# A recurrent-memory attention block with its gradients: another issue order for the backward chain, and a fixed order for the last stage's first transfers

## The chip, the cores and the metric

The kernel runs on one core of a Trainium2 chip, in one launch. The metric is the time of that launch on the device in microseconds (us), and smaller is better. TensorE is called PE here, VectorE DVE, ScalarE ACT, GpSimd POOL and SyncE SP; PE, DVE, ACT and POOL compute, and SP, ACT and POOL issue DMA transfers from queues of their own.

## The reference

The forward pass adds three things: the input, an attention with a memory that is carried from segment to segment, and a squared-ReLU MLP. The attention and the MLP both read the layer-normalised input. The sequence has S = 2048 rows of D = 512 in bf16; there are 32 heads of 128, 64 segments of 32 rows, a memory of 8 rows and an MLP width of 1792.

```
mem = mem0
for s in range(64):
    h = concat([mem, xn[32*s : 32*s + 32]])          # 40 rows
    q, k, v = h @ Wq, h @ Wk, h @ Wv                 # 32 heads of 128
    p = softmax(mask(q @ k.T * 128 ** -0.5))
    o = (p @ v) @ Wo
    mem, out[s] = o[:8], o[8:]                       # the next segment starts from mem
y = x + out + (relu(xn @ w1 + b1) ** 2 @ w2 + b2)
```

The kernel returns y and, for a given gradient of y, the gradients of x, mem0, Wq, Wk, Wv, Wo, w1, b1, w2 and b2. The memory makes both directions chains: no segment's forward can end before the one ahead of it, and the gradient of a segment needs the gradient of the memory that the segment behind it received.

## The kernel before

**Stages.** The kernel first does the MLP and the layer norm (to about 267 us of the profiled span), then the rows of the memory (the "left" rows) of all blocks together, then the forward chain of 64 segments (to about 1200 us). It then does the backward of the memory rows' own part and the MLP weight gradients (to about 1435 us), then the backward chain, again 64 segments (about 1435 to 2431 us), and at the end the last stage, which forms the four attention weight gradients and the input gradient (from 2508 us).

**The backward chain.** A segment is a step; four steps make a block, sixteen blocks in all, and both are taken from the last to the first. `bwd(s)` makes the operations of a step and `left(b)` those of a block; each has a short name. In a step: `o0mm` and `o1mm` project the incoming gradient GT through Wo; `o0ev`, `o0fl` and `o0te` copy that out, transpose it and copy again (p = 0 and 1 are halves of the heads); `s0` and `s1` are the score gradients; `d10` to `d41` are the DVE operations of the softmax gradient, which end in gS; `tu0` and `tu1` turn gS into gST; `vp`, `kp` and `qp` are the outer products for the gradients of v, k and q in PSUM tile b_pp (two of them, `pp0` and `pp1`, which the three share in turn); `vea`, `kea0`, `qea1` and so on copy these out to gv, gk, gq (names with `l`, such as `kla0`, copy the memory rows' part, b_gkL); `vg`, `kg` and `qg` gather them through the transposed weights into ps_gR; `ra` and `rb` copy that to R; `ta` and `tb` transpose R into ps_sum; and `HT` adds the four groups into GT, which is what the next step starts from. `ldp`, `ldq`, `ldn`, `ldk` and `vtr` load the next step's data, `pb` and `vc` are POOL copies. A block's operations: `L.G0` to `L.I3` are the gathers (ps_RL) for the memory rows, `L.ra0` to `L.ra3` sum them, `L.ta`, `L.tb` and `L.xt` turn them into b_XL, `L.sl` and `L.sx` store, and `L.ktr`, `L.vtr` and `L.qtr` transpose the gradients gkL, gvL and gqL of the memory rows by DMA into gNat, which `L.kst`, `L.vst` and `L.qst` store to S_GL.

All of this is issued in the order written out by hand in `B_ORDER` (L1088 to L1103), inside a manual schedule in which no tool reorders anything: four strings, for the steps 0, 1, 2 and 3 of a block (called rows 0 to 3 here). Most of row 0 stands at the end of the fourth string, one block ahead, and the first string holds only how it ends. A `+` or `-` behind a name moves it to the block or step before or after. `ENGS` (L1104) says which copies ACT does; its second string names those of DVE. Each engine runs its own instructions in order, so an instruction that waits holds all behind it on its engine.

**The last stage** (L1393 to L1506) works through 16 groups of columns, `COLS`: each is 160 products of 128 x 128 by 128 x 512 (L1503), eight results in PSUM in the case of Wo (the first group, where all eight are run side by side) or one after another. A group of Wo's gradient needs a tile `gn` of the projected output rows (S_ON, S_OL; loaded by POOL, L1419 and L1425) and GOc, the gradient rows; the others need a `gn` transposed by DMA from S_GB on SP's queue (L1422) and HNc, the rows of the normalised input. `slot_side` makes GOc and HNc: four DMA transposes on ACT's queue (L1407) and four plain copies (L1410). `loads(i)` fetches the tile for group i, two groups ahead; there are three such tiles. `leave` copies a result out of PSUM through a tile wt (six buffers) and stores it from POOL's queue. Behind each group `input_rows` (L1441 to L1471) takes a block of the input's gradient: POOL loads XT (L1444) and XL, PE transposes XT into ps_rows (L1456) and DVE and POOL finish it.

**What sets the order here.** The tile framework lets a scheduler choose the order of this stage outside a manual schedule. A transpose by DMA on one queue waits until those issued from the other queue have all landed; a framework rule adds that wait. Two transposes that write the same tile name (gNat) wait for each other's reader.

Of the kernel before, what the change touches and what calls it, by code (L numbers as in the profile page):

```python
# [10 lines left out]
BF16 = mybir.dt.bfloat16  # L11
F32 = mybir.dt.float32
P = 128
# [13 lines left out]
def kernel(  # L27
# [27 lines left out]
    nc = tc.nc  # L55

    _, S, D = A_x.shape
    M = A_mem0.shape[1]
# [4 lines left out]
    L = M + SEG  # L63
# [26 lines left out]
    gflat = grad_out.flatten_outer_dims()  # L90
# [5 lines left out]
    dma = nc.sync.dma_start  # L96
# [5 lines left out]
    NB = NSEG // SPB  # L102
    HG = 4
    KH = H // HG
# [10 lines left out]
    S_XN = dram.tile([S, D], BF16, name="S_XN")  # L115
    S_GT = dram.tile([P, DC, S], BF16, name="S_GT")

    S_HT = dram.tile([P, DC, S], BF16, name="S_HT")
    S_HX = dram.tile([S // P, P, DC, P], BF16, name="S_HX")
    S_XL = dram.tile([P, DC, S // SEG * M], BF16, name="S_XL")  # L120
    S_GM = dram.tile([P, DC, S], BF16, name="S_GM")
# [19 lines left out]
    S_GL = dram.tile([NB, HG, SEG, 3, GW], BF16, name="S_GL")  # L141
# [15 lines left out]
    def sb(name, bufs, side=None):  # L157
        return tc.tile_pool(name=name, bufs=bufs, side=side, reuse_waits="tile")

    def psum(name, bufs):  # L160
        return tc.tile_pool(name=name, bufs=bufs, space=bass.MemoryType.PSUM, reuse_waits="tile")
# [8 lines left out]
    HT = htp.tile([P, DC, S], BF16, name="HT")  # L170
# [237 lines left out]
    def turned_heads(W):  # L408

        return lambda h: W[:, :, h * P:(h + 1) * P]  # L410
# [166 lines left out]
    def on_engines(act, vec):  # L577

        return dict([(n, acp) for n in act.split()] + [(n, vcp) for n in vec.split()])
# [43 lines left out]
    with sb("fw", 1) as fw, psum("fr", 4) as fr, psum("fpp", 1) as fpp, \  # L623
# [26 lines left out]
        def big(name):  # L650
            return fr.tile([P, 512], F32, name=name, tag="r")
# [285 lines left out]
    with sb("la", 2) as la, sb("ls", 2) as ls, sb("lo", 1) as lo_, sb("wg", 2) as wg, psum("lpp", 1) as lpp, psum("lr", 4) as lr:  # L937
# [84 lines left out]
        side, part = {}, {}  # L1022
# [53 lines left out]
        with tc.manual_schedule():  # L1076
# [3 lines left out]
            for b in range(NB + 1):  # L1080
                for nm in LB_ORDER:
                    k = nm.rstrip("-")
                    c = b - (nm != k)
# [2 lines left out]


    B_ORDER = (  # L1088
        "rb tb ta ldk HT",
        "L.H2 L.ktr L.gl+ klb1- o0mm o1mm kla1- L.ra1 vc- o0ev o0fl xt- o0te vp0 s0 d10 o1ev vla vea d20 vp1 o1fl vg0 "  # L1090
        "d30 o1te s1 vtr vlb d40 kp0 tu0 d11 d21 d31 veb d41 qp0 vg1 tu1 keb0 L.sl- kea0 qeb0 kg0 kla0 qea0 vc qp1 "
        "kp1 klb0 kla1 qea1 keb1 qeb1 kea1 ldq qg0 qg1 klb1 kg1 L.I2 ra rb tb ta pb L.kst HT",
        "xt- L.I3 o0mm ldn- o0ev o1mm o0fl o1ev L.vtr o0te vp0 L.ra2 L.G3 ldk- s0 vea vp1 d10 o1fl d20 vla L.vst vtr "
        "vg0 d30 d40 veb vtr+ tu0 kp0 o1te qp0 vc klb0 s1 L.qtr vg1 vlb keb0 qeb0 qea0 ldp d11 d21 d31 d41 kea0 qg0 "
        "tu1 kp1 ldq ldp+ kla0 ldk pb L.ldt+ kea1 qp1 ldn kg0 keb1 klb1 qea1 kg1 L.qst qeb1 qg1 rb L.H3 tb ra L.ra3 "
        "ta HT",
        "o0mm o0ev o1mm L.gs+ vc o0fl kla1- o1ev vp0 o1fl xt- vp1 L.ldv+ o0te o1te s0 vea d10 d20 veb d30 s1 d40 vlb "
        "vg0 tu0 L.I0+ kp0 L.vo1+ d11 d21 vla d31 ldq kea0 L.lq+ d41 klb0 kla0 qp0 keb0 qeb0 vg1 pb qea0 kg0 qg0 tu1 "
        "kp1 qp1 L.G0+ keb1 L.vo0+ kea1 qeb1 kg1 qea1 L.qo0+ qg1 ra rb L.H0+ L.ko0+ tb klb1 ta HT L.ta L.ra0+ L.tb "
        "o0mm+ kla1 o0ev+ o1mm+ o1ev+ ldn vp0+ o0fl+ vea+ vp1+ L.xt o1fl+ o0te+ vla+ veb+ o1te+ s0+ d10+ vg0+ d20+ "  # L1100
        "d30+ d40+ ldk xt L.qo1+ s1+ L.ldk+ vlb+ L.sx+ L.ko1+ tu0+ vg1+ kp0+ d11+ kea0+ d21+ keb0+ d31+ L.I1+ klb0+ "
        "qp0+ ldn+ L.G1+ L.G2+ d41+ qea0+ tu1+ kg0+ qeb0+ kla0+ qp1+ ldp+ qg0+ ldq+ vtr+ qea1+ kp1+ qeb1+ kea1+ ldp++ "
        "qg1+ pb+ keb1+ kg1+ ra+ L.H1+")  # L1103
    ENGS = on_engines(  # L1104
        "L.ra0 kea0 keb0 keb1 kla0 kla1 o0ev o1ev qea0 qeb0 rb vea veb vla vlb",
        "kea1 klb0 klb1 o0te o1te qea1 qeb1 ra")
    with sb("bq", 1) as bq, sb("bt", 1) as bt, sb("bs", 2) as bs, sb("be", 1) as be, psum("bpp", 1) as bpp, psum("br", 4) as br:
        G4 = {n: bq.tile([P, HG, KH, SPB, SEG], BF16, name="g" + n) for n in "vkq"}
        gS = bq.tile([P, KH, KW], BF16, name="gS")
# [28 lines left out]
        def left(b):  # L1138
            B_ = block(b)
            ps, st, o = {}, {}, {}  # L1140
            src = {"v": "gvL", "k": "gkL", "q": "gqL"}
            o["lq"] = lambda: dma(B_["gqL"][:], S_GQL[b])

            def following(f):

                return lambda: f(b - 1) if b > 0 else None
            for n, f in loads.items():
                o[n] = following(f)
            o["gs"] = lambda: dma(S_GM[:, :, b * P:(b + 1) * P], gts[b][:])
            for t, n in enumerate("qkv"):  # L1150
                for x in range(2):
                    def so(n=n, t=t, gs=slice(2 * x, 2 * x + 2) if n == "v" else slice(0, HG),
                           ks=slice(0, KH) if n == "v" else HALF[x]):
                        dma(S_GB[b, t][:, gs, ks], G4[n][:, gs, ks].rearrange("p g k j r -> p g k (j r)"))
                    o["%so%d" % (n, x)] = so

            jobs = [(turned_heads(Wqkv[t]), src[n], k) for t, n in ((2, "v"), (1, "k"), (0, "q")) for k in range(KH)]
            for i in range(4):
                for x, nm in enumerate("GHI"):
                    def G_(i=i, x=x):  # L1160
                        if ("R", i) not in ps:
                            ps["R", i] = big("ps_RL")
                            ps["n", i] = 0
                        ps["n", i] += 1
                        for m, (W, n, k) in enumerate(jobs[6 * i + 2 * x:6 * i + 2 * x + 2]):
                            for g in range(HG):
                                nc.tensor.matmul(ps["R", i][32 * g:32 * g + 32, :].rearrange("p (a b) -> p a b", b=P),  # L1167
                                                 lhsT=B_[n][:, k, g, :], rhs=W(g * KH + k), start=(ps["n", i] == 1 and m == 0),
                                                 stop=(ps["n", i] == 3 and m == 1), tile_position=(0, 32 * g))
                    o["%s%d" % (nm, i)] = G_  # L1170
                if i == 0:
                    o["ra0"] = lambda: ENGS["L.ra0"](B_["R4"][:], ps["R", 0][:])
                else:
                    o["ra%d" % i] = lambda i=i: nc.vector.tensor_tensor(out=B_["R4"][:], in0=ps["R", i][:],
                                                                        in1=B_["R4"][:], op=ALU.add)
            turn_ops(o, big, lambda: B_["R4"], st)

            def xt():
                st["XL"] = bt.tile([P, DC, SPB, M], F32, name="b_XL", tag="XL")
                left_sums(st["XL"], st["T"])  # L1180
            o["xt"] = xt
            o["sl"] = lambda: dma(S_XGL[b], st["XL"][:])

            for t, n in enumerate("qkv"):
                def nt(n=n):
                    st[n] = bt.tile([P, KH, P], BF16, name="gNat", tag="gNat")
                    nc.sync.dma_start_transpose(st[n][:], B_[src[n]][:].rearrange("p k g r -> p k (g r)"))
                o[n + "tr"] = nt
                o[n + "st"] = lambda n=n, t=t: dma(S_GL[b].rearrange("g r t c -> (g r) t c")[:, t, :],
                                                   st[n][:].rearrange("p k e -> p (k e)"))  # L1190

            o["sx"] = lambda: dma(S_XG[b], B_["XT"][:].rearrange("p c j r -> p c (j r)"))
            return o

        pre, gts, loads = {}, {}, {}
# [161 lines left out]
        with tc.manual_schedule():  # L1357
# [3 lines left out]
            for b in range(NB):  # L1361
                lefts.append(left(b))
# [34 lines left out]
    with sb("p5a", 1) as p5a, sb("p5h", 1) as p5h, sb("p5", 2) as p5, sb("p5g", 1) as p5g, \  # L1397
# [6 lines left out]

        def slot_side(t_, srcT, src):
            for dc in range(DC):
                nc.scalar.dma_start_transpose(t_[:, 0:NB, dc * P:(dc + 1) * P], srcT[:, dc, :])  # L1407
            lv = src.rearrange("(c q r) d -> c q r d", q=16, r=SEG)
            for c in range(NLC):
                nc.scalar.dma_start(t_[:, NB + c, :], lv[c][:, 0:M, :])  # L1410
            return t_

        def rows_of(i, g, blocks, left_):
# [19 lines left out]
        def loads(i):  # L1433
            if i < len(COLS):
                t, g = COLS[i]
                if t == 3:
                    got[i] = rows_of(i, g, None, lambda g: S_OL[:, g])
                else:
                    got[i] = rows_of(i, g, lambda b: S_GB[b, t], lambda g: S_GL[:, g, :, t, :])
# [40 lines left out]
        p5g.tile([P, 896], BF16, name="gap5")  # L1480
        GOc = p5g.tile([P, RC_ALL, D], BF16, name="GOc")
        side = p5h.tile([P, RC_ALL, D], BF16, name="HNc")
        loads(0)
        slot_side(GOc, S_GM, gflat)
        loads(1)
        slot_side(side, S_HT, S_XN[:])
        for i, (t, g) in enumerate(COLS):
            loads(i + 2)
            gn = got[i]
# [52 lines left out]
```

## Time and profile before

The median of three runs is 3085.69 us (3084.45 to 3087.76). One profiled execution spans 3081.8 us.

| what | us |
|---|---|
| PE busy | 2698.1 (88% of the span) |
| PEld busy | 1389.7 (45%) |
| DVE busy | 1332.6 (43%) |
| ACT busy | 973.0 (32%) |
| POOL busy | 659.1 (21%) |
| a step of the backward chain, mean | 15.1 |
| from the chain's last PE work to the first ps_gw | 2431.8 to 2508.3 |
| the last stage's first group, then each later one | 36.16, about 34.97 with its ps_rows |

How to read it: the engines' busy times are shares of the same span and overlap; PEld is the loading of weights, which goes beside the matmuls. A row such as `PE ps_gw L1503 <- DMA GOc<-S_GM: 76.5, 1, 76.5` among the waits says that the operation on PE which writes ps_gw, at line 1503, waited 76.5 us for a DMA transfer into GOc from S_GM, once. In the chain of waits, "SPq" is SP's queue, in which a transfer's issue stands.

### The profile page before, as it was taken

The page shows a single profiled execution, that of the slowest core. Times are in us where ns is not written, and L with a number is a line of the kernel's source. Part 1 is how long each engine was busy: PE and PEld are TensorE (multiplying, and loading weights), DVE is VectorE, ACT ScalarE, POOL GpSimd, SP SyncE. Part 2 cuts the span into 40 slices and gives each one's busy share as a digit, 9 for nine tenths or more (in the row PEclk, how much of TensorE's full clock was granted, in tenths as well). Part 3 has the DMA queues.
Part 4 walks back from the last instruction along what each step waited for, and adds up shares of the span by engine and source line. Part 5 has one row for each costly group of instructions (what it writes and reads, how often), then busy time and mean ns, then how long its engine had stood idle before and what let it go on. Part 6 is the DMA issues. An engine that isn't in the chain of part 4 may idle for free.

```text
span 3081.8 us, 109732 instructions
## 1 busy us (share of the span) xinstructions
PE 2698.1 (88%) x48600; PEld 1389.7 (45%) x48600; DVE 1332.6 (43%) x3645; ACT 973.0 (32%) x2242; POOL 659.1 (21%) x1264
## 2 busy tenths in 40 slices
PE   7997899999999886877888888888888449999998
PEld 4453444444444444455444444444444214444443
DVE  5442566666665664433454445444544201100010
ACT  2322444444444444333333333333333101111111
POOL 0000000000000000223333333333333203322222
PEclk9998999999999998998999999999999779999999
DMA  9548376867667577777567777777777879999991
GB/s 255 184 150 243 110 178 169 193 171 181 183 173 186 144 172 205 229 236 208 144 161 186 181 172 168 193 183 169 171 192 175 234 153 200 239 206 211 213 197 39
DMA packets 794558, 566.77 MB, mean 184 GB/s; under 512 B 579409, under 2 KB 681570, under 8 KB 790754
## 3 DMA queue, kind: packets, MB, share of 16 engines
q1 hardware_dynamic: 734130, 426.80, 58.7%
q0 software_dynamic: 40528, 126.53, 14.4%
q10 hardware_dynamic: 19424, 6.42, 0.9%
q8 instruction: 381, 6.24, 0.9%
q14 instruction: 95, 0.78, 0.1%
HBM read 193.61 MB, written 238.56 MB: 140 GB/s over the span
## 4 chain that ended last, share of the span: by engine, by line
PE 71%; DVE 13%; DMA 5%; issue 4%; SPq 3%; ACT 3%; POOL 1%; ACTq 0%; DVEq 0%; POOLq 0%
PE ps_gw L1503 18%; PE ps_proj L392 13%; PE ps_gR L460 9%; PE ps_R L460 4%; PE ps_L L350 3%; PE ps_sum L469 3%; PE b_pp L547 3%; PE ps_tr L165 2%; PE ps_w L1045 2%; PE ps_w L1039 2%; PE ps_RL L1167 1%; PE f_pp L547 1%; PE ps_sc L437 1%; SPq L1422 1%; PE ps_ga L279 1%
## 5 line engine op out<-in xcount | busy, mean ns | idle before, releaser
L1503 PE MATMUL ps_gw<-gn,HNc 128*128 128x512 bf16 x1920 | 416.4, 379 | 0.0
L1503 PEld LDWEIGHTS <-HNc 128*128 128x128 bf16 x1920 | 187.9, 98 | 223.8
L374 ACT CAST f_N<-ps_proj 128x512 bf16<-128x512 f32 x320 | 186.1, 582 | 243.9 <-PE ps_proj L392 228.1
L1475 ACT CAST wt<-ps_gw 128x512 bf16<-128x512 f32 x128 | 74.4, 587 | 516.1 <-PE ps_gw L1503 385.1
L392 PEld LDWEIGHTS <-X 128*32 128x32 bf16 x6144 | 153.4, 97 | 161.4 <-DVE X L482 14.1
L1458 DVE TENSOR_TENSOR gx<-ps_rows,gb 128x512 f32<-128x512 f32 x16 | 11.1, 692 | 455.3 <-PE ps_rows L1456 455.3
L1503 PE MATMUL ps_gw<-GOc,gn 128*128 128x512 bf16 x640 | 140.2, 382 | 76.5 <-DMA GOc<-S_GM 76.5
L835 POOL COPY kM<-f_kT 128x256 bf16<-128x256 bf16 x64 | 25.8, 403 | 786.2 <-DVE f_kT L377 570.3
L460 PE MATMUL ps_gR<-Wq,gq 128*32 128x512 bf16 x2048 | 149.1, 393 | 19.2 <-DVE gq L377 10.6
L374 ACT CAST gk<-b_pp 128x256 bf16<-128x256 f32 x192 | 68.9, 376 | 274.8 <-PE b_pp L547 190.9
L460 PE MATMUL ps_gR<-Wk,gk 128*32 128x512 bf16 x2048 | 144.4, 397 | 2.4 <-issue 1.7
L392 PE MATMUL ps_proj<-Wk,X 128*32 128x512 bf16 x2048 | 135.4, 384 | 12.5 <-DVE X L482 6.9
L392 PE MATMUL ps_proj<-Wo,GT 128*32 128x512 bf16 x2048 | 124.0, 384 | 14.0 <-DVE GT L482 7.3
L460 PE MATMUL ps_gR<-Wv,gv 128*32 128x512 bf16 x2048 | 135.5, 385 | 0.6 <-issue 0.5
L1503 PEld LDWEIGHTS <-gn 128*128 128x128 bf16 x640 | 62.9, 98 | 152.6 <-issue 78.8
L392 PE MATMUL ps_proj<-Wq,X 128*32 128x512 bf16 x2048 | 128.8, 382 | 0.0
L469 PE MATMUL ps_sum<-identF,R 128*128 128x128 f32 x512 | 92.6, 291 | 39.6 <-ACT R L374 35.7
L1238 POOL COPY PD<-b_P 32x320 bf16<-32x320 bf16 x256 | 115.3, 451 | 49.3 <-DMA b_P<-S_A 41.4
L1476 POOL DMA_DIRECT2D out_dram<-wt x128 | 69.4, 543 | 262.4 <-ACT wt L1475 256.5
L460 PE MATMUL ps_R<-Wo,OT 128*32 128x512 bf16 x2048 | 125.3, 385 | 0.0
L392 PE MATMUL ps_proj<-Wv,X 128*32 128x512 bf16 x2048 | 124.1, 378 | 0.0
L1251 POOL COPY b_vT<-b_vl 128x1024 bf16<-128x1024 bf16 x64 | 66.4, 1038 | 260.7 <-PE ps_sc L437 192.7
(260 smaller groups left out, 5147.9 us busy)
## 6 DMA issues: line engine op xcount, KB each, us to landing
S_A<-f_N SPq DMA_DIRECT2D x64, 512.0 KB
out_dram<-wt POOLq DMA_DIRECT2D x142, 128.0 KB, 4.9
S_A<-f_N SPq DMA_DIRECT2D x64, 256.0 KB
S_GB<-gv SPq DMA_DIRECT2D x32, 512.0 KB
S_GB<-gq SPq DMA_DIRECT2D x32, 512.0 KB
S_GB<-gk SPq DMA_DIRECT2D x32, 512.0 KB
b_kN<-S_A POOLq DMA_DIRECT2D x63, 256.0 KB, 4.4
b_qN<-S_A POOLq DMA_DIRECT2D x63, 256.0 KB, 4.2
```

Of the source, the lines that this page charges most:

```text
L165: nc.tensor.transpose(ps_ap, in_ap, ident[base:base + k, base:base + k])
L350: nc.tensor.matmul(ps[:], lhsT=x(dc), rhs=Wqkv[t][:, dc, c0:c0 + 512], start=(dc == 0), stop=(dc == DC - 1))
L374: nc.scalar.copy(out, in_)
L392: nc.tensor.matmul(o, lhsT=hT[:, dc, :], rhs=x, start=(dc == 0), stop=(dc == DC - 1), tile_position=(0, 32 * g))
L460: nc.tensor.matmul(o, lhsT=XT(k, g), rhs=x, start=(first and k == 4 * h), stop=(last and k == 4 * h + 3), tile_position=(0, 32 * g))
L469: nc.tensor.transpose(st["T"][:, c * P:(c + 1) * P], R4()[:, c * P:(c + 1) * P], identF[:])
L547: nc.tensor.matmul(o, lhsT=N_[32 * g:32 * g + m, kk * P:(kk + 1) * P], rhs=X(kk)[32 * g:32 * g + m], start=(i == 0), stop=(i == len(jobs) ...
L1238: nc.gpsimd.tensor_copy(PD[32 * g:32 * g + 32, g], C["P"][32 * g:32 * g + 32, :, 0:L])
L1251: nc.gpsimd.tensor_copy(vT[:, :, :, 0:SEG], C["vl"][:])
L1475: nc.scalar.copy(wt[:], ps[:])
L1476: pdma(dst, wt[:])
L1503: nc.tensor.matmul(ps[:], lhsT=l(rc), rhs=r(rc), start=(n == 0), stop=(n == RC_ALL - 1))
```

## The change

The aim is to shorten the backward chain by a different order of issue, searched over a model of the engines in which instruction fetch comes later than before, and to start the last stage earlier by giving its first transfers a fixed order. It has three parts.

1. `B_ORDER` is written anew, and `qea1`, one of the copies of the gradient of q, goes from DVE to ACT.
2. In the last block processed (b = 0) the transposes and stores `ktr`, `vtr`, `qtr`, `kst`, `vst`, `qst` go to ACT's queue, and the three transposes take three different tiles (gNat, gON, gOT), so that none waits for another's store.
3. `slot_side` issues from SP's queue instead of ACT's, and the first two `loads` and both `slot_side` calls are put in a manual schedule, so that they are issued as written.

```diff
     ENGS = on_engines(
-        "L.ra0 kea0 keb0 keb1 kla0 kla1 o0ev o1ev qea0 qeb0 rb vea veb vla vlb",
-        "kea1 klb0 klb1 o0te o1te qea1 qeb1 ra")
+        "L.ra0 kea0 keb0 keb1 kla0 kla1 o0ev o1ev qea0 qea1 qeb0 rb vea veb vla vlb",
+        "kea1 klb0 klb1 o0te o1te qeb1 ra")
...
                 def nt(n=n):
-                    st[n] = bt.tile([P, KH, P], BF16, name="gNat", tag="gNat")
-                    nc.sync.dma_start_transpose(st[n][:], B_[src[n]][:].rearrange("p k g r -> p k (g r)"))
+
+                    tag = "gNat" if b > 0 else {"k": "gNat", "v": "gON", "q": "gOT"}[n]
+                    st[n] = bt.tile([P, KH, P], BF16, name="gNat", tag=tag)
+                    (nc.sync if b > 0 else nc.scalar).dma_start_transpose(st[n][:], B_[src[n]][:].rearrange("p k g r -> p k (g r)"))
                 o[n + "tr"] = nt
-                o[n + "st"] = lambda n=n, t=t: dma(S_GL[b].rearrange("g r t c -> (g r) t c")[:, t, :],
+                o[n + "st"] = lambda n=n, t=t: (dma if b > 0 else nc.scalar.dma_start)(S_GL[b].rearrange("g r t c -> (g r) t c")[:, t, :],
                                                    st[n][:].rearrange("p k e -> p (k e)"))
...
             for dc in range(DC):
-                nc.scalar.dma_start_transpose(t_[:, 0:NB, dc * P:(dc + 1) * P], srcT[:, dc, :])
+                nc.sync.dma_start_transpose(t_[:, 0:NB, dc * P:(dc + 1) * P], srcT[:, dc, :])
             for c in range(NLC):
-                nc.scalar.dma_start(t_[:, NB + c, :], lv[c][:, 0:M, :])
+                dma(t_[:, NB + c, :], lv[c][:, 0:M, :])
...
-        loads(0)
-        slot_side(GOc, S_GM, gflat)
-        loads(1)
-        slot_side(side, S_HT, S_XN[:])
+        with tc.manual_schedule():
+            loads(0)
+            slot_side(GOc, S_GM, gflat)
+            loads(1)
+            slot_side(side, S_HT, S_XN[:])
```

The four main strings of `B_ORDER`, cut to the part from the first k product on, where the orders differ most (before, then after; rows 1, 2, 3 and 0):

```diff
 row 1
-kp0 tu0 d11 d21 d31 veb d41 qp0 vg1 tu1 keb0 L.sl- kea0 qeb0 kg0 kla0 qea0 vc qp1
-kp1 klb0 kla1 qea1 keb1 qeb1 kea1 ldq qg0 qg1 klb1 kg1 L.I2 ra rb ta tb pb L.kst HT
+kp0 vc tu0 vtr+ o1te ldp qp0 qeb0 s1 qea0 d11 d21 kea0 keb0 d31 vg1 qg0 kla0
+klb0 d41 kg0 kp1 tu1 kea1 qp1 L.I3 keb1 qeb1 kg1 qea1 qg1 rb ra L.I2 L.vtr tb ta HT
 row 2
-kp0 o1te qp0 vc klb0 s1 L.qtr vg1 vlb keb0 qeb0 qea0 ldp d11 d21 d31 d41 kea0 qg0
-tu1 kp1 ldq ldp+ kla0 ldk pb L.ldt+ kea1 qp1 ldn kg0 keb1 klb1 qea1 kg1 L.qst qeb1 qg1 rb L.H3 tb ra L.ra3 ta HT
+kp0 veb tu0 o1te keb0 qp0 s1 qea0 klb0 vg1 kea0 kla0 pb d11 d21 kg0 L.sl-
+d31 vc d41 tu1 qeb0 kp1 qp1 keb1 qg0 qea1 L.gl+ kea1 kg1 qeb1 qg1 rb ra tb ta L.H3 kla1 HT
 row 3
-kp0 L.vo1+ d11 d21 vla d31 ldq kea0 L.lq+ d41 klb0 kla0 qp0 keb0 qeb0 vg1 pb qea0 kg0 qg0 tu1
-kp1 qp1 L.G0+ keb1 L.vo0+ kea1 qeb1 kg1 qea1 L.qo0+ qg1 ra rb L.H0+ L.ko0+ tb klb1 ta HT L.ta L.ra0+ L.tb
+kp0 ldk- kla0 qp0 vg1 d31 kea0 keb0
+d41 kg0 qea0 qeb0 qg0 tu1 kp1 klb0 qp1 kea1 L.vo1+ qeb1 L.G0+ pb keb1 qea1 kg1 qg1 kla1 L.vo0+ rb L.ldk+
+L.ta L.tb tb ra ta L.lq+ HT L.H0+ L.ra0+ L.xt
 row 0 (begins at the end of the fourth string, ends in the first)
-kp0+ d11+ kea0+ d21+ keb0+ d31+ L.I1+ klb0+
-qp0+ ldn+ L.G1+ L.G2+ d41+ qea0+ tu1+ kg0+ qeb0+ kla0+ qp1+ ldp+ qg0+ ldq+ vtr+ qea1+ kp1+ qeb1+ kea1+ ldp++
-qg1+ pb+ keb1+ kg1+ ra+ L.H1+ rb tb ta ldk HT
+kp0+ ldk veb+ d11+ d21+ xt ldn+ tu0+ keb0+ d31+ ldp+ L.G1+ vg1+ L.qo1+ qp0+ L.sx+ kea0+
+L.ko1 kg0 d41 qea0 L.G2 qeb0 tu1 qg0 kla0 qp1 klb0 L.I1 qea1 qeb1 kp1 qg1 keb1 kea1 klb1 kg1 rb ra L.H1
+tb kla1 vtr ta ldq HT
```

## The prediction

> **What bounds the kernel now.** I read the slices of the span first, then the waits of PE over the backward chain, then the chain of work around the hand-over to the last stage, then engine and DMA load there by windows. A tenth of load is a tenth of a slice of 77 us.
>
> ```profile
> PE   7997899999999886877888888888888449999998
> ...
> PEclk9998999999999998998999999999999779999999
> DMA  9548376867667577777567777777777879999991
> ```
>
> PE is the bound nearly everywhere. The backward chain (1435 to 2431 us) shows an 8: 937.3 us pass between the first and the last of 63 GT updates spaced one step apart (1473.0 to 2410.3), 15.1 a step, with 128.6 us in which PE stands still between 1440 and 2432. The two 4s and the clock of 7 are the hand-over. Where the chain's idle time goes:
>
> ```profile
> PE ps_sum L469 <- ACT R L374: 27.4, 48, 1.0
> PE b_pp L547 <- DVE b_gkL L377: 19.7, 35, 0.6
> PE ps_gR L460 <- DVE gq L377: 10.6, 15, 1.7
> PE b_pp L547 <- ACT b_gkL L374: 9.6, 16, 0.6
> PE b_pp L547 <- DVE gk L377: 9.5, 16, 0.6
> PE b_pp L547 <- issue: 9.2, 16, 1.5
> PE ps_proj L392 <- DVE GT L482: 7.3, 19, 0.4
> ```
>
> The columns are total us, number, longest. No wait is long; each is a copy out of PSUM that comes a fraction of a microsecond late (48 waits on R, one in most steps). Order alone can shorten them, by standing PE work from elsewhere in front.
>
> The hand-over, in the chain of work (start, us, what):
>
> ```profile
> 2431.34 0.45 PE ps_m L1388 x4
> 2431.79 2.60 SPq L1422
> 2434.44 10.73 SPq L1422
> 2445.27 0.57 SPq L1189
> 2445.89 14.92 SPq L1422
> ...
> 2474.33 4.47 DMA GOc<-S_GM
> 2478.82 1.23 SPq L1422
> 2480.09 3.86 DMA gn<-S_GB
> 2484.03 4.31 DMA GOc<-S_GM
> ...
> 2502.76 5.32 DMA GOc<-S_GM
> 2508.32 36.16 PE ps_gw L1503 x160
> ```
>
> From 2431.8 PE has nothing: its first product wants GOc, whose four pieces are DMA transposes on ACT's queue. They alternate with gn transposes (for the third column group, needed 70 us later) on SP's queue, each starting only when the other queue's has landed. By windows (PE, PEld, DVE, ACT, POOL busy; clock; DMA share; GB/s):
>
> ```profile
> 2440.00:2450.00 10.00, 0.00 (x0) 0.00 (x0) 0.00 (x0) 0.00 (x0) 2.50 (x4) 0.50 1.07 336
> 2450.00:2470.00 20.00, 0.00 (x0) 0.00 (x0) 0.00 (x0) 0.00 (x0) 1.66 (x3) 0.50 1.06 295
> 2470.00:2490.00 20.00, 0.00 (x0) 0.00 (x0) 0.00 (x0) 0.00 (x0) 0.00 (x0) 0.50 0.60 122
> ```
>
> Until 2467 the DMA engines are full: POOL's loads of column groups 0 and 1 (10.5 MB). After that they are half idle and the hand-over is pure latency.
>
> **What the Trainium skill says.** "DMA: Bandwidth & Descriptors", section "Silent corruption: two transposing streams in flight at once": transposes of SP and of ACT must be kept apart, the later stream waiting for the earlier one's completion. The trace agrees: gn at 2480.1 follows GOc (2474.3 to 2478.8), four turns of 9.4 to 9.7 us. Same page, "Queues, rings and completion order": a DMA engine takes turns between queues by packet. It agrees: beside POOL's packets (4096 B, 167 ns each) the 256 B transpose packets (18 ns) got some 0.11 of the time, so 256 KB took 10.7 to 14.9 us, against 3.9 alone. "TensorE: Matmul & The Clock Gate", "What's actually happening": an idle window of about 3.4 us halves the clock and a like busy window restores it. It agrees: clock 0.50 above, and the first group took 36.16 us where 34.53 is a later one's matmul time, 1.6 lost.
>
> **Part 1, the chain's order.** I followed PE's instructions step by step in both orders, with the durations of the trace (projection 1.91 us a step, a gather of 16 matmuls 0.91, of 8 0.46, copies 0.21 to 0.44, GT 0.29), asking at each wait what PE now has in front. PE idle by step of a block before: 0.99, 1.33, 2.88, 2.11 us (steps at rows 1, 2, 3 and 0 of the order), 7.3 in 60.6.
> - Row 1 takes L.I3's 16 matmuls of 56 ns over from row 2, and its second q outer product waits for kea1 on DVE: 0.46 + about 0.6 = +1.1.
> - Row 2: loses these (−0.46), but shows more of its R copy: −0.35.
> - Row 3: had 15.2 us in 30 waits of b_pp on gST, 7.8 on R, 5.7 on GT over the 15 blocks, 1.9 a block. Now one copy instead of three stands between kp0 and qp0, L.ta and L.tb fill the R wait and L.H0 the GT wait: −1.4.
> - Row 0: qea1's copy goes to ACT beside qeb1 on DVE, and L.I1 stands between qp1 and qg1, so the gq wait (12.9 us in 15, 0.86 each) goes; G1 and vg1 between kp0 and qp0 cover 0.4 of gST: −1.25.
>
> Sum −1.9 a block, 15.5 blocks: −29. That is the good end: it assumes no copy queues behind another, and DVE and ACT change their order too. The bad end is +15 (1 us a block: row 1 as walked, and only the 0.1 of rows 2, 3 and 0 taken together coming back). I take about half of the good end, −15, because row 1's new wait is certain in the order whereas the gains rest on several copies each coming in time.
>
> **Part 2, the hand-over.** Removed: the alternation. POOL's loads(0) no longer stand behind loads(1), whose first load waited for the last ps_RL (19.5 us, POOL), so their packets start near 2422.5, not 2432, and 10.5 MB are through near 2461, not 2467. For the last block ktr, kst, vtr, vst, qtr and qst are on ACT's queue in tiles of their own, so vtr needn't wait for kst's store. GOc and HNc are on SP, one stream. Then, with the trace's pieces: ktr starts near 2428 and vtr, both crawling beside POOL's packets, lands near 2462; two gn (still ahead of GOc0, waiting for vtr) and GOc0 in one stream 7.7 (gn 3.9 with the second a packet time behind, GOc 3.8 to 4.5) → 2469.7; qtr on ACT is one change of stream, 3.9 → 2473.6; GOc1 to 3 in one stream, 4.4 and then about 2.5 each → 2483. Before: 2508.3. So −25. Bounds: if vtr crawls to 2467 and GOc follows at 4.4 each, 2492, −16; if the transposes run ahead of POOL's bulk, 2475, −33. The 14 gn now stand behind HNc; they are needed at about 2553 and want 14 × 1.3 us at the rate of the trace's back-to-back ones: free. Eight more ps_RL after the last R: 8 × 56 ns = +0.45.
>
> Added: input_rows' first loads (XT, XL). Before, POOL issued XT at 2492.47, and ps_rows ran with no gap after group 1 (2544.5). In the changed order they stand behind group 1's eight output stores; wt has six buffers, so copies 7 and 8 wait for stores to land (in the trace the first store went at 2544, the eighth copy at 2548.5, and a transfer issued then needed 7.5 to 7.9 us: 2552.85 to 2560.37). PE meets ps_rows right behind group 1, and the products of group 2 are queued behind it. XT would be issued about 5 us after the group's end, on landing 3 (as at 2492, DMA quiet) to 7.9 later: a stall of 8 to 13, plus 0.5 to 1.6 for the clock; I take +12.5, since the loads for group 3 fill the DMA then. Later input_rows are a group behind and hidden, and so is the DVE copy of XL.
>
> Hand-over: −25 + 0.5 + 12.5 = −12. From −33 + 9 = −24 to −16 + 15 = −1.
>
> **Rivals.**
> - *Chain order brings nothing*: the waits only move from one copy to another; for it: row 1's new wait, and waits of 0.2 to 0.6 us spread over seven causes, which no single edit removes; against: 12.9 us of gq waits lose their cause. −12 alone: 3073.7.
> - *All of it comes*: XT lands in time or the DMA is quiet (no stall), chain −25: 3085.7 − 25 − 25 = 3036. For it: 0.50 to 0.60 DMA share at such moments before; against: POOL's issue order.
> - *Slower*: the chain's bad end, +15, with the poor end of the hand-over, −16 + 0.5 + 8 = −7.5: 3093; with the stall at 15, 3100. For it: PE is the bound already, every step's order changed, and a copy that comes late in one step delays the recurrence itself; against: the causes removed in rows 3 and 0.
>
> **How the numbers follow.** Main, −12 − 15 = −27: 3059, chance 0.54. Nothing from the chain 3074, 0.18. All of it 3036, 0.14. Slower 3093, 0.14. The range 3036 to 3081 leaves the slower case and the best of the "all" case out. Faster by over 6 us: main, all and most of the second, 0.82; same 0.06; slower 0.12.
>
> **What would show it.** GT intervals of about 14.9 us instead of 15.1; no wait of 0.86 of ps_gR on gq in row 0 and a new one of about 0.6 in row 1; first ps_gw near 2483 − 15 = 2468; a wait of ps_rows on XT of 8 to 13 us behind group 1, absent before; gn transposes never between two GOc. A first ps_gw within 5 us of the chain's end + 76 as before, or chain intervals over 15.1, would prove it wrong.

## The result, and the profile after

The changed kernel takes 3061.11 us (median of four runs, 3051.72 to 3068.14) where the kernel before took 3085.07 beside it (3082.38 to 3087.76): ratio 0.992, interval 0.9892 to 0.9949, so 24 us less. One profiled execution spans 3059.8 us, 22.0 less than the one before. Its slices, as on the page of before:

```profile
PE   8997899999999886877799899998989559999998
...
PEclk9998999999999998999999999999999879999999
DMA  9548375766767767777577676776777899898991
```

The hollow at the hand-over is 5 and 5 where it was 4 and 4, and part of the chain shows 9 instead of 8. With the same marks as before (us of the profiled span):

| | before | after | difference |
|---|---|---|---|
| first to last GT update of the chain | 937.3 | 918.3 | −19.0 |
| last PE work of the chain to the first ps_gw | 76.5 | 54.8 | −21.7 |
| first ps_gw to PE's last work | 561.1 | 578.1 | +17.0 |

Three smaller terms, the start of the chain 2.4 us later, the stretch from the last GT to the chain's end 0.2 shorter and the time behind PE's last work 0.3 shorter, make up the rest. PE's waits in the chain (total us, number, longest), as shown for before:

```profile
PE ps_gR L460 <- ACT gk L374: 12.9, 30, 0.5
PE b_pp L547 <- issue: 11.6, 5, 2.7
PE ps_sum L469 <- ACT R L374: 10.1, 19, 0.5
PE b_pp L1290 <- POOL PD L1239: 10.0, 11, 1.4
...
PE b_pp L547 <- DVE gk L377: 9.3, 16, 0.6
```

The waits on R fell from 27.4 to 10.1, the 19.7 for b_gkL from DVE and the 10.6 for gq from DVE are gone. In their place stand waits on gk from ACT, and one that was not there before: on PD, which POOL copies. The wait of b_pp on gk from DVE looks unchanged (9.5 before, 9.3 after, 16 times), but before it stood in row 2 and now it stands in row 1.

The chain of work at the hand-over (start, us, what):

```profile
2409.55 20.80 DMA gNat<-b_gkL
2430.37 0.35 ACTq L1190
2431.05 16.92 DMA gNat<-b_gvL
2448.03 1.31 SPq L1423
2449.38 1.31 SPq L1423
2451.05 4.79 DMA GOc<-S_GM
2456.00 3.06 DMA gNat<-b_gqL
2459.07 2.40 SPq L1408
...
2464.82 4.76 DMA GOc<-S_GM
2469.82 35.03 PE ps_gw L1505 x153
...
2514.72 0.51 POOL XT L1445
2515.23 4.98 DMA XL<-S_XGL
2520.72 1.09 PE ps_rows L1457 x4
```

The four turns between gn and GOc have become one, for qtr (gqL). What remains is two slow transposes, ktr and vtr, 37.7 us together, then one line of single transfers. At the bottom is the new stall: PE ends group 1 at 2506.35 and idles 14.4 us until XT and XL, issued behind the stores, have landed. Among PE's waits it is this line:

```profile
PE ps_rows L1457 <- DVE XT L1448: 14.4, 1, 14.4
```

### The profile page after: what moved, and what is told of

Its sections match the earlier page's. It is cut to its first block, busy times and chain, and to the rows that moved or that the text cites. A ratio compares the mean times of both kernels' runs of the same rounds, so it can differ in the third digit from the quotient of the medians.

```text
span 3059.8 us, 109712 instructions
## 1 busy us (share of the span) xinstructions
PE 2705.4 (88%) x48600; PEld 1386.8 (45%) x48600; DVE 1319.5 (43%) x3581; ACT 994.7 (33%) x2306; POOL 658.0 (22%) x1264
## 5 line engine op out<-in xcount | busy, mean ns | idle before, releaser
L392 PEld LDWEIGHTS <-X 128*32 128x32 bf16 x6144 | 153.3, 97 | 161.3 <-DVE X L482 13.9
L1505 PE MATMUL ps_gw<-GOc,gn 128*128 128x512 bf16 x640 | 142.2, 385 | 54.8 <-DMA GOc<-S_GM 54.8
L460 PE MATMUL ps_gR<-Wk,gk 128*32 128x512 bf16 x2048 | 146.7, 386 | 19.4 <-ACT gk L374 12.9
L460 PE MATMUL ps_gR<-Wq,gq 128*32 128x512 bf16 x2048 | 141.6, 382 | 1.2 <-issue 1.2
L469 PE MATMUL ps_sum<-identF,R 128*128 128x128 f32 x512 | 102.4, 295 | 24.6 <-ACT R L374 18.4
L374 ACT CAST gON<-ps_proj 128x512 bf16<-128x512 f32 x128 | 74.9, 585 | 143.2 <-PE ps_proj L392 141.5
```

The lines of the kernel that those rows point to most:

```text
L374: nc.scalar.copy(out, in_)
L392: nc.tensor.matmul(o, lhsT=hT[:, dc, :], rhs=x, start=(dc == 0), stop=(dc == DC - 1), tile_position=(0, 32 * g))
L460: nc.tensor.matmul(o, lhsT=XT(k, g), rhs=x, start=(first and k == 4 * h), stop=(last and k == 4 * h + 3), tile_position=(0, 32 * g))
L469: nc.tensor.transpose(st["T"][:, c * P:(c + 1) * P], R4()[:, c * P:(c + 1) * P], identF[:])
L1505: nc.tensor.matmul(ps[:], lhsT=l(rc), rhs=r(rc), start=(n == 0), stop=(n == RC_ALL - 1))
```

## The experiments

All kernels compute the whole reference. The kernel before ran between 3075 and 3102 us beside the experiments, so each is judged by its ratio to it; for the reader, 0.001 is 3.1 us.

**Part 1 alone, and parts 2 and 3 alone.** The first is the kernel before with the new `B_ORDER` and `ENGS`, the second the changed kernel with the old ones.

> The kernel before with the new B_ORDER and with qea1 on ACT, nothing else. Theory (the three terms add up: chain -19 between first and last GT update, hand-over -22, stall of ps_rows +15): GT updates 918 us apart as in the changed kernel, the old alternation of gn and GOc, no stall behind group 1, so 3085 - 17 = 3068, from 3062 to 3073. Rival (the chain's gain needs the new hand-over, or came from elsewhere): 3080 or more, with GT updates over 930 us apart.

> The changed kernel with the old B_ORDER and with qea1 on DVE: parts 2 and 3 alone. Theory: GT updates 937 us apart, then 22 us less from the chain's end to the first ps_gw, then a stall of ps_rows of about 15 behind group 1: 3085 - 7 = 3078, from 3073 to 3082. Rival (the transfers were hidden anyway or the stall eats all): 3084 to 3090. Other rival (no stall without the new order, which moved it): 3063.

Part 1 alone: 0.995 (0.9931 to 0.9968), GT updates 920.5 apart, 78.3 us to the first ps_gw, no stall. Parts 2 and 3 alone: 0.9966 (0.995 to 0.9983), GT updates 938.2 apart, 52.1 us to the first ps_gw, then a stall of 13.9. Both are what the theories expected, read by the ratio (some 15 and 10 us). The two together make −26 us at 3089, the changed kernel 24: the gains add up, as far as intervals of some 5 us on either side tell. The stall comes with parts 2 and 3, whatever the order of the chain.

**The stall behind group 1.**

```diff
+            ahead = fetch(NB - 1)        # XT, XL, gb, xn, gi of the first input_rows, behind slot_side(side, ...)
...
-            input_rows(NB - 1 - i)
+            input_rows(NB - 1 - i, ahead if i == 0 else None)
```

> The changed kernel with the five loads of the first input_rows issued in the manual schedule behind HNc's transfers, so ahead of group 1's stores on POOL. Theory (POOL's order makes the stall, 14.3 us of PE's time): no wait of ps_rows on XT, 3061 - 14 = 3047, from 3044 to 3051. Rival (PE would wait there for HNc or the next gn tile instead, or the clock's fall costs it): 3055 or more.

0.9881 (0.9861 to 0.9902), some 12 us under the changed kernel's 0.992, and 16 under the 0.9932 that it had in the later repetition below. PE has no gap in the last stage, which lasts 561.1 us again against 578.1. So POOL's order made the stall. Part of the gain went back at once: the first ps_gw came 60.5 us after the chain's end, not 54.8. The early loads ran beside the last GOc transpose, which took 8.97 us instead of 4.76, and vtr had hardly changed:

```profile
2441.93 17.61 DMA gNat<-b_gvL
...
2476.19 8.97 DMA GOc<-S_GM
```

**Group 1's loads out of the way of the transposes.**

```diff
-            q = pdma if i < 2 else dma
+            q = pdma if i < 1 else dma
```

> As the kernel with early XT loads, and the loads of column group 1 (5.25 MB) go to SP's queue behind GOc instead of POOL's. Theory (the transposes of gkL and gvL crawl because POOL's loads of group 1 fill the DMA engines beside them): vtr takes about 4 us instead of 17, the first ps_gw starts some 14 us earlier, 3033, from 3029 to 3038. Rival (they are bound by loads of group 0 or by the turns between queues): the same as without, within 4 us; or group 1 now waits for its own tile, and what is gained at the start is lost at the second group.

0.9857 (0.9837 to 0.9877). The chain of work shows vtr freed, and what took over:

```profile
2415.77 19.50 DMA gNat<-b_gkL
...
2435.97 3.47 DMA gNat<-b_gvL
...
2461.71 6.62 DMA GOc<-in_grad_out_dram
2468.34 37.46 PE ps_gw L1510 x160
```

vtr takes 3.47 us where it took 17.61 with early XT loads alone; ktr stays at 19.5, and group 0's loads, beside which it runs, were not moved. The wait of PE fell from 60.5 to 47.1 us, about the 14 that were expected. The time did not follow in full: by the ratios it fell by 7 us, to some 3041 (of 3085) and not 3033, and since the two intervals overlap, this step alone is not resolved. In the profiles 3.4 us are lost again behind PE's last work (15.4 us, where it was 12.0) and 1.3 in the last stage; why wasn't looked into. The transposes do starve beside POOL's loads, as the prediction had it.

**Part 2 taken back** (the last block's transposes and stores on SP again, in one tile; part 3 kept).

> The changed kernel without part 2: in the last block too the transposes and stores of gkL, gvL and gqL are on SP's queue and share one tile. Theory (one queue for all transposes is what counts, and part 2 gives only the missing waits for stores): no turns between queues at all, but vtr and qtr each wait for a store to land and hold SP's queue; the first ps_gw comes from 5 us earlier to 10 us later after the chain's end than the 54.8 of the changed kernel. Rival (part 2 is half of the gain): 65 us or more.

0.9882 (0.986 to 0.9904), 3047.6 us: better than the changed kernel. PE waits 62.1 us for the first product, so part 2 gains 7.3 us there: inside the theory's span (49.8 to 64.8), toward its slow end and not far under the rival's 65. But PE has no gap behind group 1: in this kernel's order XT's load stands ahead of the stores again (issued at 2459.5, the first store at 2509.8), and the last stage lasts 562.0 us. Part 2's own gain of 7 is paid for with the stall that it brings beside part 3, 16 us in the last stage. So the fixed order of part 3 does not bring the stall by itself. Why the scheduler puts XT's load behind the stores when part 2 is there too, and what part 2 does without part 3, wasn't tried.

**The hand-over, further.** With group 1's loads on SP and early XT loads as above, and: the third group's gn behind HNc, GOc's plain copies ahead of its transposes, the early loads on SP, and the last block's qtr in row 0.

```diff
-        "... qp1 klb0 L.I1 qea1 qeb1 kp1 ..."
+        "... qp1 klb0 L.I1 L.qtz qea1 qeb1 kp1 ..."      # L.qtz: qtr of the last block alone
...
+            ahead = fetch(NB - 1, dma)
+            loads(2)
```

> On top of the early XT loads and of group 1's loads on SP's queue: the third group's gn transposes stand behind HNc, GOc's plain copies ahead of its transposes, the early XT loads on SP's queue behind HNc, and the last block's qtr (its source is loaded from memory and doesn't need the chain's end) is issued in row 0, before the bulk loads. Theory (what is left between vtr and the first product is a chain of single steps: two gn, GOc0, the turn to ACT for qtr, three GOc, their copies): from 47.1 us to about 33 after the chain's end, 3033 where the kernel with early XT loads and group 1 on SP gives 3047. Rival (bound by the bulk loads): 43 or more.

0.9839 (0.9813 to 0.9864), 3032.16 us. The time is the 3033 that the theory named, but beside a kernel before that ran some 8 us shorter than in the last comparison. By the ratios it is 5 to 6 us less than with group 1 on SP alone, with intervals that overlap. The wait fell from 47.1 to 39.7 us, not to 33:

```profile
2408.61 23.08 DMA gNat<-b_gkL
2431.77 0.35 ACTq L1191
2432.16 7.40 DMA gNat<-b_gvL
2439.58 2.70 DMA S_GL<-gNat
...
2442.40 0.69 DVE gm L1392
2443.11 0.31 SPq L1393
...
2447.85 4.60 DMA GOc<-S_GM
...
2452.59 0.59 PE ps_gw L1513
```

The turns are gone: no other transpose comes between GOc's four, and the last lands 9.3 us after the store of gm is issued. But ktr and vtr took 30.5 us together where they took 23.0 in the kernel with group 1 on SP. And a link shows that was hidden before: gm (the gradient of mem0) is copied into vtr's tile, so it waits for vtr's store, and its own store stands on SP's queue ahead of GOc's last three transposes.

**The chain: PD's copies earlier.** Row 1's new wait on PD, tried from two sides. First the copies themselves:

```diff
-  (row 0)  kg1 rb ra L.H1 ...        (row 1)  L.ra1 vc- pb- o0ev
+  (row 0)  kg1 rb ra pb L.H1 ...     (row 1)  L.ra1 vc- o0ev
```

> The changed kernel with row 1's copies of P into PD (pb) issued in row 0 ahead of L.H1, not behind vc- in row 1. Theory (row 1's waits of b_pp on PD, 10.0 us in 11 of the changed kernel's profile, come from pb standing behind vc on POOL): the waits on PD go, row 1 about 0.6 shorter a block, 10 us less than the changed kernel. Rival (pb waits for its data or the wait passes to another copy in row 1): row 1's median step the same within 0.2 us.

1.0023 (1.0009 to 1.0038): slower than the kernel before. POOL now waits for the load of P with vc behind it:

```profile
POOL PD L1239 <- DMA b_P<-S_A: 70.5, 18, 8.0
```

In the changed kernel it was

```profile
POOL PD L1239 <- DMA b_P<-S_A: 19.4, 14, 2.9
```

PE's waits on PD did not go (13.0 us in 11), it gets a new one of ps_sc on b_vT, 18.4 us in 15, and row 1 goes from 14.42 to 16.44 us. So the load was late and not the copy, and the copies that were issued earlier held up what stands behind them on POOL. Then the load, ahead of k's, whose wait for a free buffer had held it:

```diff
-        "d21+ xt ldn+ tu0+ keb0+ d31+ ldp+ L.G1+ ..."
+        "d21+ xt ldp+ ldn+ tu0+ keb0+ d31+ L.G1+ ..."
```

> The changed kernel with ldp+ (the load of P for row 1) issued ahead of ldn+ on POOL in row 0, not behind it. In the trace pb of row 1 starts when that load lands, and the load is issued only when ldn+'s buffer has come free. Theory (the late load makes row 1's waits on PD, 7 to 10 us): these waits fall under 2 us, row 1 about 0.5 shorter, 5 to 10 us less than the changed kernel (0.990 of the kernel before). Rival (pb is then held by vc on POOL, or k's load comes late in its place): the same within 3 us, or new waits on b_kN.

The wait on PD is gone from PE's list, and row 1 takes 13.81 us (14.42 and 14.22 in two profiles of the changed kernel). The time is 0.991 (0.9888 to 0.9933) beside 0.9932 and 0.992 of the changed kernel: less or the same, not resolved. GT updates are 916.5 apart.

**The chain: qea1 and L.I3.**

```diff
-    "... qea0 qea1 qeb0 rb ...", "... o1te qeb1 ra"
+    "... qea0 qeb0 rb ...", "... o1te qea1 qeb1 ra"
```

> The changed kernel with qea1 back on DVE, B_ORDER as changed. Theory (ACT taking qea1 is what ends the wait of ps_gR on gq in row 0): gq waits come back in row 0, up to 0.86 a block, row 0's median step 15.4 or more against 14.87, some 8 to 13 us slower than the changed kernel. Rival (the order did it, with L.I1 and kp1 in front of qg1): row 0 within 0.2 us, and the time the same.

```diff
-kp1 tu1 kea1 qp1 L.I3 keb1
+kp1 tu1 kea1 L.I3 qp1 keb1
```

> The changed kernel with L.I3 ahead of qp1 in row 1 instead of behind it. Theory (row 1's second q product waits about 0.6 for kea1 on DVE, and 0.46 of work in front of it would cover most of that): row 1's waits on gk of DVE, 9.3 us in 16, fall to 2 or 3, 7 us less than the changed kernel. Rival (qp1 later only makes its copies later, and the wait shows at qg1 or R): row 1's median step within 0.15 us.

> The changed kernel itself, for comparison with the other three: 3061 or what the chip's own level makes of 0.992 of the kernel before, GT updates 918 us apart; how far an execution's chain can differ with the same order is read from it, up to 931 in one profile with the same chain.

The changed kernel, again: 0.9932 (0.9915 to 0.9948), GT updates 924.9 apart. qea1 back on DVE: 0.9902 (0.9887 to 0.9916), so 9 us faster by the ratios, 7.5 by the medians, and not slower; GT updates 909.4 apart. Its row 0 is longer, 15.10 against 14.86 us by the median; row 2 is shorter, 13.65 against 14.04, which is 6 us over 16 blocks. Row 1 is at 13.92 against 14.15, less than it differs between the two profiles of the changed kernel (14.49 and 14.15). None of row 0's waits on gq came back (the one of 0.6 us on gq in its list stands ahead of the first GT update). L.I3 first: 0.9913 (0.9897 to 0.9929), GT updates 917.5 apart; the wait of b_pp on gk of DVE fell from 9.3 us in 16 to 0.6 in one, but 3.6 us of new waits of ps_gR on gk (16 times) show in row 1, whose median is 14.14 against 14.15. The rival's reading of the row holds: the wait was passed on. The difference in time is not resolved, as the two intervals overlap.

**All of it together:** the further hand-over, qea1 on DVE, L.I3 first and P's load first.

> The kernel with the further hand-over (early XT loads, group 1 on SP, qtr early, gn behind HNc), and in the chain qea1 back on DVE, L.I3 ahead of qp1 and ldp+ ahead of ldn+. Theory (the edits work on different rows and stages, so they add up: 0.984 for the hand-over, some 9 us for qea1, 4 to 6 for the other two): 0.979 of the kernel before, from 0.976 to 0.981, GT updates 900 to 908 us apart. Rival (the chain's edits share one wait, or shift the stalls of instruction fetch to a worse place): 0.983 or more.

0.9804 (0.9784 to 0.9824), 3029.91 us: inside the range, and of the kernels tried the lowest ratio, though its interval overlaps that of the further hand-over alone. The chain is the part that did not come as expected: GT updates 917.0 apart, not 900 to 908. Rows 1 and 2 kept their gains (medians 13.68 and 13.65), and row 0 lost (15.28 against 14.87 and 14.86 in the changed kernel's two profiles). Row 3, 15.59, lies between the 15.02 and 15.89 of these two.

## Why the prediction was right

**The sum.** It forecast 3059 and 3061.11 came. Its two terms were −15 (chain) and −12 (hand-over with the stall). The first profile has −19.0 and −21.7 + 17.0 = −4.7; the second profile of the same kernel (GT updates 924.9 apart, 55.8 us to the first ps_gw, a last stage of 577.8) has −12.4 and −4. So the chain's term is right within what two profiles differ by, and the hand-over's was too good by 7 to 8 us, of which 3 to 4 are the first ps_gw and some 4 the stall. That the total came within about 2 us is in part luck. By times and not profiles, part 1 alone took 15 us off and parts 2 and 3 alone 10, which is nearer to the two terms.

**The chain by rows**, mean us between GT updates:

| row | before | after | forecast | measured | qea1 on DVE |
|---|---|---|---|---|---|
| 1 | 13.42 | 14.42 | +1.1 | +1.00 | 14.00 |
| 2 | 14.19 | 14.05 | −0.35 | −0.14 | 13.70 |
| 3 | 16.88 | 15.85 | −1.4 | −1.03 | 15.89 |
| 0 | 16.16 | 15.00 | −1.25 | −1.16 | 15.19 |

The measured columns are of one profile each; the second profile of the changed kernel has 14.22, 14.04, 16.41 and 15.11, so row 3 is known to half a microsecond only. The sum is −1.33 of the −1.9 that was called the good end; taking half of it was a little low. Row 1's cost is the sum as forecast, and the wait for kea1 is there (9.3 us in 16, 0.58 each). But two terms that the walk left out cancelled: the wait on PD (10.0 us in the row) came, and the wait on R (9.2 us in row 1 of before) went. Row 2 fell short because of qea1: with it on DVE the row takes 13.70, −0.49. Two readings were off without harm: L.I3 has 8 matmuls and not 16 (the 0.46 in the sum is right for 8), and row 3's waits "of b_pp on gST", 15.2 us, are in the trace waits for the copies b_gkL, 18.1 us in 30.

**The step that failed** is row 0's cause. The prediction divided 12.9 us of gq waits by 15 blocks, 0.86 each, and gave them to qea1's place on ACT beside qeb1, and to L.I1. Taken one by one, the 15 waits are of two kinds: nine of 0.24 to 0.57 us, and six of 1.2 to 2.6, 9.9 us in all. One of each, the wait in square brackets (before):

```profile
1530.22 1.04 PE L460 MATMUL ps_gR<-Wq,gq 128*32 128x512 bf16 x14 [1.67 <-DVE gq L377]
1590.14 1.04 PE L460 MATMUL ps_gR<-Wq,gq 128*32 128x512 bf16 x14 [0.30 <-DVE gq L377]
```

In five of the six DVE stands idle before the copy of gq, for 1.8 to 2.2 us, where it is 0.9 to 1.4 beside the short ones, and waits for PE's product; in the sixth the copy had been done for 2.0 us. So a queue of copies on DVE did not make them. Each of the six ends 1.5 to 1.6 us after the end of a packet of the instruction queue, and these packets come some 5.5 us apart: that PE stood without instructions is likely, not shown. Only the short waits, 0.3 us a block, are of the kind that the prediction reasoned about. With qea1 back on DVE none of them came back, and row 0 rose by 0.24 us only, so the new order removed them (the prediction had named L.I1 of it) and not the engine. The long ones have left row 0 as well, but in the changed kernel five of 2.0 to 2.7 us, 11.6 in all, stand in row 3, where before had three of 1.4 to 1.8:

```profile
1692.74 0.21 PE L547 MATMUL b_pp<-gST,b_kN 32*128 32x32 bf16 x4 [2.58 <-issue]
```

What else made row 0 shorter are the waits on b_gkL (8.9 us in 15, gone, more than the 0.4 a block that was put there) and on R (8.3 in 15, gone, and not in the sum), against new ones on gk of ACT (7.8 in 15). So it is in good part luck that −1.16 lies near the forecast of −1.25. The change of engine was a loss on the whole, 7 to 9 us.

**The hand-over.** First ps_gw at 2468 was forecast, 2469.8 came; measured from the chain's end it is 54.8 us against 51, and the rest is the chain's larger gain. vtr's landing was put 30.2 us behind the chain's end, and was 33.0. The two gn with GOc0 took 7.8 us (7.7 forecast), qtr 3.1 (3.9), GOc1 to 3 10.5 (9.4). The crowding by POOL's packets was shown by moving half of them away (vtr 17.61 to 3.47).

**The stall** was of the right kind and undersized: 14.4 us without PE work and 1.5 for the second group at first at the lower clock (36.06 us, 34.53 at full clock), 15.9 where 12.5 was taken. The mis-sized term is the issue of XT: 8.4 us after group 1's end, not about 5, as the seventh copy out of PSUM, and the eighth behind it, waited 4.5 us for an earlier store to land. The landing took 5.0, inside the 3 to 7.9. The two pages of the Trainium skill that bore on these steps still agree with the trace. As "DMA: Bandwidth & Descriptors" has it for two transposing streams (section "Silent corruption: two transposing streams in flight at once"), qtr on ACT starts (2456.0) only when GOc0 on SP has landed (2455.84), while SP's two gn and GOc0, one stream, follow each other without a turn. As "TensorE: Matmul & The Clock Gate" has it for an idle PE (section "What's actually happening"), the clock stood at 0.50 from 2430 to 2469, until the first product.

## What to carry to other kernels

An issue order searched for one stretch moves waits to places that no edit names; compare the waits by cause and by step before and after, not the busy shares. Look at single waits before dividing a sum by its count: here a mean of 0.86 us was nine waits of about 0.3 and six long ones of another kind, and long ones stand elsewhere under the new order. When some transfers get a fixed order and others another queue, look at what the scheduler then does with those left free: here a load that was needed after 37 us went behind eight stores, and that ate most of what the hand-over had gained. A move of one copy to another engine is worth a run of its own: here it was a loss inside a gain.

## What was not expected of the hardware

- The same program's chain took 918.3 and 924.9 us in two profiles, and 930.8 and 922.0 in two kernels with the same chain; times of the changed kernel spread over 16 us. PE stops for 2.0 to 2.7 us in row 3 of five blocks (the 1st, 4th, 7th, 11th and 14th) in the changed kernel's profile, each stop ending 1.2 to 1.6 us after the end of a packet of the instruction queue, which come some 5.5 us apart (166 over the chain); in before the six stops of row 0 (blocks 1, 4, 5, 8, 11 and 14, of 1.2 to 2.6 us) end 1.5 to 1.6 us after one. That they are instruction fetch is suggested by this and was not tried.
- Loads needed some 45 us later stood beside a 512 KB transpose that took nearly twice as long (8.97 us, 4.76 without them), and a bulk load beside one of 256 KB made it five times as long (17.61 us, 3.47 without).
